# Loading q and k two batches ahead and transposing them with the DMA crossbar

**Chip, cores, metric.** One core of one Trainium2 chip. The metric is device time of one launch in microseconds (us), median of several runs.

## The reference

Two stages: attention in a window of 32 tokens on either side, with 8 global tokens, and a feed-forward layer on its result.

```python
# q, k, v: (8 batches, 8 heads, 576 tokens, 64)
scores = scale * (q @ k^T)                       # scale = 1/8
mask = (|i - j| <= 32) | is_global[i] | is_global[j]
attn = softmax(where(mask, scores, -1e9))
x = (attn @ v).transpose(0, 2, 1, 3).reshape(4608, 512)
h = x @ w_in                                     # 512 -> 2048: "first layer"
s = sin(alpha * h)
g = h + s * s / (alpha + 1e-9)
out = g @ w_out                                  # 2048 -> 512: "second layer"
```

## The kernel before

It goes through the batches in a loop. **Part p** is the attention of batch p, with the second-layer matmuls of token chunk p-1 as filling between its steps. **First-layer part p** follows: the 16 slots of the first layer of chunk p, each 4 matmuls, a sine on ScalarE, a square and an add. What the next batch needs is prepared in the meantime:

- GpSimd (called POOL in the profile) issues the loads of q, k and v of batch p+1 early in part p; `with_extra` hangs four on each of the first steps.
- TensorE transposes q and k of batch p+1, head pair by head pair, during the later attention steps of part p. VectorE copies transposed k and ScalarE copies transposed q out of PSUM, the memory that TensorE writes to.
- Sync, in slot 10 of first-layer part p, shifts v: it copies v within SBUF into a second arrangement and adds the rows of the global tokens. The V matmuls of part p+1 read that. Below, "the shift" stands for these four DMAs, two shifts and two copies of global v. `VW` has two buffers: the loads of v issued in part p fill the one that the V matmuls of part p do not read.

```python
def shift_v(b, eng=nc.sync):
    W = VW[b % 2].rearrange("p a h u d -> p a h (u d)")
    eng.dma_start(out=W[0:64, 1], in_=W[QB : QB + 64, 0])
    eng.dma_start(out=W[64:KB, 1, :, 0 : (NU - 1) * D], in_=W[64 - QB : KB - QB, 0, :, D:])

def global_v(b):
    # ... two more Sync DMAs into the same VW, from VgX

def T_half(src, b, hp, out):                      # TensorE transposes, one head pair
    for jt in range(NTW):
        for t, pr in heads:
            nc.tensor.transpose(out=out[pr, jt * TW : (jt + 1) * TW],
                in_=src[:, 2 * hp + t, jt, :], identity=identb[0:TW, 0:TW])

# ... the loop over p, part p:
    at = {2 + hp: [T_(p + 1, hp)] for hp in range(NHP)}
    parts = attention(p, psA, at)
    if p + 1 < B:
        with_extra(parts, load_slots(p + 1), 0, 4)
        # ... gathers and copies of the global tokens on GpSimd
    run(parts, counts, fill)
# ... first-layer part p:
    m1 = mm1(p, H2[p], psB, sq_last if p == B else sq_first if p == 0 else sq_late)
    vs = [partial(shift_v, p + 1), partial(global_v, p + 1)]
    m1[10] = partial(chain, m1[10], *vs)
```

`sq_late` says which engine squares which slot; nearly all are on GpSimd.

The softmax here doesn't subtract the row's maximum and nothing guards it: scores larger than these inputs give would overflow.

## Time and profile before

| | before |
|---|---|
| time, median | 359.7 us (358.81 to 361.65, 4 runs; the 360.4 of the prediction is the median of the first 3) |
| TensorE busy | 94% of the profiled span of 356.8 us |
| parts 2 to 6 (from the load of the Exp table to the first `hb` matmul) | 21.9 us each (part 4: 23.3, with an idle moment of 1.2 us in it) |
| first-layer parts 2 to 6 | 14.8 to 15.1 us each |

The prediction below reads the page. One thing that it uses is not shown there: when Sync shifts v, and when the result is needed. The timeline lists, for a group of instructions on one engine, start, duration, engine, line, operation, operands and count; a bracket at the end would be idle time of the engine ahead of it and what released it. First Sync in first-layer part 5, then TensorE early in part 3:

```profile
227.82 0.55 SPq L143 DMA_DIRECT2D VW<-VW  x1
228.43 0.66 SPq L144 DMA_DIRECT2D VW<-VW  x1
229.13 1.60 SPq L152 DMA_DIRECT2D VW<-VgX  x2
```

```profile
133.94 1.04 PE L703 MATMUL o<-w_out,H2b 128*128 128x512 bf16 x4
134.91 0.44 PE L553 MATMUL num<-E,VW 120*64 120x56 bf16 x16
```

The first V matmul (`num<-E,VW`) comes about 5 us into its attention part.

### The profile page before, as it was taken

How to read it: one execution, taken by the hardware profiler on the slowest of the kernel's cores; microseconds unless marked ns; L12 is line 12 of the kernel's file. 1: busy time of each engine (PE TensorE's matmuls, PEld its weight loads, DVE VectorE, ACT ScalarE, POOL GpSimd, SP SyncE). 2: the span in 40 equal slices, each digit the busy share in tenths (PEclk: the TensorE clock that was granted, in tenths of full speed). 3: DMA queues.
4: the chain of work that ended last, by engine and by line, in shares of the span. 5: the costliest groups of instructions: out<-in, count | busy, mean ns of one | idle time of the engine just before them, and what ended most of it. 6: DMA issues, size and time to landing. Idle time of an engine off the chain costs nothing.

```text
span 356.8 us, 9407 instructions
## 1 busy us (share of the span) xinstructions
PE 336.7 (94%) x3738; PEld 172.0 (48%) x3738; DVE 237.4 (67%) x527; ACT 245.9 (69%) x376; POOL 205.6 (58%) x302
## 2 busy tenths in 40 slices
PE   6686997999999999999989999999999999999996
PEld 5563444444455445544554446444544444444444
DVE  5765784758775687668764878487848764875610
ACT  3756885847894889578975888488848884844401
POOL 9858897355871787169805791579247205755000
PEclk9999999999999999999999999999999999999999
DMA  9999999940598429940995099409931001001012
GB/s 75 166 196 184 199 170 179 182 136 20 35 171 104 112 17 168 122 114 3 165 115 134 2 121 154 136 8 90 181 105 43 30 32 61 0 2 59 31 59 88
DMA packets 133149, 35.39 MB, mean 99 GB/s; under 512 B 121794, under 2 KB 126818, under 8 KB 133106
## 3 DMA queue, kind: packets, MB, share of 16 engines
q0 software_dynamic: 123120, 20.04, 77.5%
q1 hardware_dynamic: 9682, 14.63, 13.9%
q8 instruction: 29, 0.48, 0.5%
q10 hardware_dynamic: 304, 0.14, 0.1%
q14 instruction: 14, 0.11, 0.1%
HBM read 38.95 MB, written 9.44 MB: 136 GB/s over the span
## 4 chain that ended last, share of the span: by engine, by line
PE 65%; ACT 13%; DMA 7%; POOL 6%; issue 4%; DVE 3%; POOLq 1%; ACTq 0%; DVEq 0%
PE hb L664 28%; PE o L703 12%; PE ops L703 12%; DMA w_out<-in_moe_w_out_dram 4%; ACT E L507 3%; PE num L553 3%; PE Sp L501 2%; DVE H2b L654 2%; ACT L607 2%; PE den L535 2%; DMA QS<-in_q_dram 2%; PE hb L703 2%; ACT Sb L671 2%; ACT lnd L541 2%; ACT L614 2%
## 5 line engine op out<-in xcount | busy, mean ns | idle before, releaser
L671 ACT ACTIVATE Sb<-hb,alphaT 128x512 bf16<-128x512 f32 x144 | 96.9, 684 | 57.6 <-PE hb L664 54.2
L664 PE MATMUL hb<-xT,w_in 128*128 128x512 bf16 x576 | 128.9, 379 | 1.6 <-POOL xT L588 1.4
L681 POOL TENSOR_TENSOR S<-Sb 128x512 bf16<-128x512 bf16 x94 | 96.0, 1041 | 48.2 <-ACT Sb L671 44.8
L654 DVE SCALAR_TENSOR_TENSOR H2b<-S,recipT,hb 128x512 bf16<-128x512 bf16 x144 | 102.4, 740 | 30.7 <-POOL S L681 30.3
L664 PEld LDWEIGHTS <-w_in 128*128 128x128 bf16 x576 | 55.7, 98 | 68.3 <-issue 1.8
L703 PEld LDWEIGHTS <-H2b 128*128 128x128 bf16 x560 | 49.6, 98 | 56.6 <-issue 2.5
L703 PE MATMUL ops<-w_out,H2b 128*128 128x512 bf16 x304 | 73.9, 380 | 1.5 <-DMA w_out<-in_moe_w_out_dram 1.5
L703 PE MATMUL o<-w_out,H2b 128*128 128x512 bf16 x224 | 54.4, 381 | 0.0
L588 POOL COPY xT<-xg 128x4 bf16 x64 | 12.9, 201 | 66.1 <-DVE xg L586 62.6
L507 ACT ACTIVATE E<-Sp 128x896 bf16<-128x896 f32 x48 | 43.5, 905 | 7.1 <-PE Sp L501 7.0
L572 DVE TENSOR_TENSOR xT<-num,rec 128x384 bf16<-128x384 f32 (+1 forms) x60 | 25.9, 453 | 23.1 <-PE num L553 18.3
L541 ACT ACTIVATE lnd<-den 128x384 f32<-128x384 f32 x48 | 23.7, 493 | 17.8 <-PE den L535 17.6
L513 DVE TENSOR_TENSOR E<-E,MASK 128x896 bf16<-128x896 bf16 x48 | 30.0, 626 | 6.4 <-ACT E L507 6.4
L553 PEld LDWEIGHTS <-VW 120*64 120x64 bf16 (+1 forms) x768 | 16.7, 114 | 20.0 <-issue 12.5
L543 ACT ACTIVATE rec<-lnd 128x384 f32<-128x384 f32 x48 | 25.1, 524 | 1.5
L501 PE MATMUL Sp<-qT,kTw 64*128 64x56 bf16 x768 | 19.7, 189 | 5.5 <-ACT qT L421 2.1
L465 DVE COPY kTw<-Kps 128x1344 bf16<-128x1344 bf16 x29 | 24.3, 839 | 0.0
L681 DVE TENSOR_TENSOR S<-Sb 128x512 bf16<-128x512 bf16 x34 | 17.6, 517 | 9.9 <-ACT Sb L671 9.8
L501 PEld LDWEIGHTS <-kTw 64*128 64x128 bf16 x768 | 15.4, 96 | 17.4 <-issue 11.5
L553 PE MATMUL num<-E,VW 120*64 120x56 bf16 (+1 forms) x720 | 20.3, 197 | 1.4 <-issue 1.2
L128 POOL DMA_DIRECT2D KS<-in_k_dram x18 | 20.7, 1152 | 0.6 <-issue 0.6
L128 POOL DMA_DIRECT2D QS<-in_q_dram x18 | 20.2, 1122 | 0.0
(133 smaller groups left out, 304.1 us busy)
## 6 DMA issues: line engine op xcount, KB each, us to landing
out_dram<-osb SPq DMA_DIRECT2D x35, 256.0 KB
KS<-in_k_dram POOLq DMA_DIRECT2D x14, 288.0 KB, 5.6
QS<-in_q_dram POOLq DMA_DIRECT2D x14, 288.0 KB, 10.2
VW<-in_v_dram POOLq DMA_DIRECT2D x12, 336.0 KB, 11.4
VW<-VW SPq DMA_DIRECT2D x7, 384.0 KB
w_in<-in_moe_w_in_dram POOLq DMA_DIRECT2D x2, 1024.0 KB, 15.3
w_out<-in_moe_w_out_dram POOLq DMA_DIRECT2D x2, 1024.0 KB, 16.0
VW<-VW SPq DMA_DIRECT2D x7, 240.0 KB
```

What stands on the lines that cost most here:

```text
L128: nc.gpsimd.dma_start(out=dst[:, h0 : h0 + nh].rearrange("p h t d -> p (h t) d"), in_=heads_ap(src, b, h0, 0, TW, 0, nh * NTW),)
L501: nc.tensor.matmul(out=Sp[:, t, m * QC : (m + 1) * QC], lhsT=kTw[hp][pr, i, :], rhs=qT[hp][pr, i, :], start=True, stop=True, skip_group_ch ...
L507: nc.scalar.activation(out=E[:], in_=Sp[:, :, 0:EW], func=AF.Exp, scale=scale)
L513: nc.vector.tensor_tensor(out=E[:], in0=E[:], in1=mk[:, None, :].to_broadcast([P, 2, EW]), op=ALU.mult)
L541: nc.scalar.activation(out=lnd[:], in_=den[:, :, 0:QB], func=AF.Ln)
L553: nc.tensor.matmul(out=num[pr, m, :], lhsT=W[0:nk, i % 2, 2 * hp + t, i // 2, :], rhs=E[0:nk, t, m * QC : (m + 1) * QC], start=b > 0 or m ...
L572: nc.vector.tensor_tensor(out=xT[:, hp, x0 : x0 + nb * QB].rearrange("p (u c) -> p u c", u=nb), in0=num[:, m0 : m0 + nb, 0:QB], in1=rec[:, ...
L654: nc.vector.scalar_tensor_tensor(out=H2b[:, n_, :], in0=s_[:], scalar=recipT[:, n_ : n_ + 1], in1=h_, op0=ALU.mult, op1=ALU.add,)
L664: nc.tensor.matmul(out=h2[:], lhsT=w_in[:, ci, nt * P : (nt + 1) * P], rhs=xT[:, ci, c * CH : (c + 1) * CH], start=(ci == 0), stop=(ci == ...
L671: nc.scalar.activation(out=Sb[:], in_=h2[:], func=AF.Sin, scale=alphaT[:, nt : nt + 1])
L681: eng.tensor_tensor(out=S2[:], in0=Sb[:], in1=Sb[:], op=ALU.mult)
L703: nc.tensor.matmul(out=ops[:], lhsT=H2b[:, nt, ts * P : (ts + 1) * P], rhs=w_out[:, nt, :], start=(nt == 0), stop=(nt == NT - 1),)
```

## The change

Its intent is to take 384 transposes off TensorE in parts 3 to 6. q and k of batches 4 to 7 are loaded two batches ahead in 12 loads of 96 tokens; Sync transposes them through the DMA crossbar (a DMA that transposes what it copies) in the first-layer part between; the attention steps of the part after then copy from SBUF. The v shift goes from slot 10 to slot 13, behind the transposes.

```diff
+    def x_loads(b):
+        # ... 12 GpSimd loads, one for each of k, q and each 96 tokens
+    def cross(b, kq, jt):
+        if jt == 0:
+            XT[kq] = qkp.tile([P, NHP, S], BF, name=("KS", "QS")[kq])
+        src = qk[b][1 - kq]
+        nc.sync.dma_start_transpose(
+            out=XT[kq][:, :, jt * TW : (jt + 1) * TW],
+            in_=src[:, jt].rearrange("p h d -> p (h d)"),
+        )
+    def stage_X(b, hp):
+        # ... three VectorE copies of transposed k, one ScalarE copy of transposed q
-                    at = {2 + hp: [T_(p + 1, hp)] for hp in range(NHP)}
+                    at = {2 + hp: [partial(stage_X, p + 1, hp) if p > 2 else T_(p + 1, hp)] for hp in range(NHP)}
-                    with_extra(parts, load_slots(p + 1), 0, 4)
+                    ld = load_slots(p + 1) if p < 3 else v_loads(p + 1, QUADS)
+                    if p > 1 and p + 2 < B:
+                        ld += x_loads(p + 2)
+                    with_extra(parts, ld, 0, 5)
-                    m1[10] = partial(chain, m1[10], *vs)
+                    if p > 1 and p + 2 < B:
+                        for i in range(2 * NTW):
+                            m1[1 + i] = partial(chain, m1[1 + i], partial(cross, p + 2, i // NTW, i % NTW))
+                    m1[13] = partial(chain, m1[13], *vs)
```

More of the change, by code (lines that the diff above doesn't have):

```diff
@@ L476, in T_Q, with rows @@
         return partial(copy, out=qT[hp][:, :, 0:QB], in_=Qps[:].rearrange("p (i c) -> p i c", c=QB))
+    XT = {}
+    def x_loads(b):
+        QS = qkp.tile([TW, NTW, H, D], BF, name="QS")
+        KS = qkp.tile([TW, NTW, H, D], BF, name="KS")
+        qk[b] = (QS, KS)
+        def rows(src, dst, jt):
+            nc.gpsimd.dma_start(
+                out=dst[:, jt],
+                in_=bass.AP(
+                    tensor=src.tensor, offset=src.offset + (b * H * S + jt * TW) * D,
+                    ap=[[D, TW], [S * D, H], [1, D]],
+                ),
+            )
+        return [partial(rows, s_, d_, jt) for s_, d_ in ((k, KS), (q, QS)) for jt in range(NTW)]
+    def cross(b, kq, jt):
[5 more added lines that the diff above has]
+            in_=src[:, jt].rearrange("p h d -> p (h d)"),
+        )
+    def stage_X(b, hp):
+        kx, qx = XT[0][:, hp], XT[1][:, hp]
+        base = kx[:, 0:1]
+        win = lambda i0, n: bass.AP(
+            tensor=base.tensor, offset=base.offset + i0 * QB - WIN,
+            ap=[list(base.ap[0]), [QB, n], [1, KB]],
+        )
+        nc.vector.tensor_copy(out=kTw[hp][:, 1 : NW - 1, 0:KB], in_=win(1, NW - 2))
+        nc.vector.tensor_copy(out=kTw[hp][:, 0, WIN:KB], in_=kx[:, 0 : KB - WIN])
+        nc.vector.tensor_copy(out=kTw[hp][:, NW - 1, 0 : KB - WIN], in_=kx[:, S - KB + WIN : S])
+        return partial(
+            nc.scalar.copy, out=qT[hp][:, :, 0:QB], in_=qx.rearrange("p (i c) -> p i c", c=QB)
+        )
     def stage_T(b, hp, pool, tag):
```

## The prediction

> **What bounds the kernel now.** I read the engine table first, then the chain of waits, then busy time by stretch. The kernel alternates parts: attention of batch p together with the second layer of token chunk p-1 ("part p"), then the first layer of chunk p ("first-layer part p"). The page says that TensorE is almost never idle and that most of the closing chain is its own work:
>
> ```profile
> PE 336.7 (94%) x3738; PEld 172.0 (48%) x3738; DVE 237.4 (67%) x527; ACT 245.9 (69%) x376; POOL 205.6 (58%) x302
> q0 software_dynamic: 123120, 20.04, 77.5%
> q1 hardware_dynamic: 9682, 14.63, 13.9%
> PE 65%; ACT 13%; DMA 7%; POOL 6%; issue 4%; DVE 3%; POOLq 1%; ACTq 0%; DVEq 0%
> ```
>
> So TensorE work taken out of a stretch in which it never waits is worth its own length, if no other engine then becomes the limit. The chain shows where parts begin (the Exp table load, L607, at 241.18 and 277.91) and where the first layer takes over (263.29 and 297.71). Busy time in part 6, which still makes transposed q, k for batch 7, and in part 7, which makes none:
>
> ```profile
> 241.18:263.29 22.11, 21.84 (x362) 11.65 (x361) 15.67 (x39) 16.91 (x26) 12.59 (x24) 1.00 1.44 122
> 277.91:297.71 19.80, 19.55 (x266) 9.25 (x264) 12.48 (x35) 14.65 (x22) 2.35 (x9) 1.00 0.12 42
> ```
>
> Columns: length, then busy PE, PE weight loads, DVE, ACT, POOL. 96 matmuls fewer, 2.29 us less TensorE time, 2.31 us less length: the part is TensorE-bound and the saving passes through. The chain of part 5 shows the unit of that cost, 12 transposes of k and 12 of q for one head pair:
>
> ```profile
> 214.16 0.26 PE Kps L456 x12
> 214.42 0.26 PE qp L456 x12
> ```
>
> 0.52 us for a pair, four pairs a batch: 2.1 us, which fits the 2.3. Last, GpSimd, because the change hangs more loads on it. In part 2:
>
> ```profile
> 93.52 1.27 POOL L128 DMA_DIRECT2D KS<-in_k_dram  x1
> 97.13 1.18 POOL L128 DMA_DIRECT2D QS<-in_q_dram  x1
> 98.29 2.57 POOL L109 DMA_DIRECT2D VW<-in_v_dram  x2
> 100.84 0.54 POOL L115 DMA_DIRECT2D VW<-in_v_dram  x1
> 105.58 0.26 POOL L448 COPY qT<-GT 128x96 bf16<-128x96 bf16 x1
> 111.82 0.46 POOL L588 COPY xT<-xg 128x4 bf16 x2 [5.97 <-DVE xg L586]
> 112.49 1.51 POOL L588 COPY xT<-xg 128x4 bf16 x6 [0.20 <-POOL xT L588]
> ```
>
> GpSimd issues 7 loads by 101.4, is free from 105.8, and waits 6 us for work. The last two lines are the global tokens' columns of xT; the compiled order shows that the first matmul of the first layer waits for GpSimd there. They end at 114.0, first-layer part 2 starts at 114.87: less than 1 us of room against them, 6 us against what lies before them on GpSimd.
>
> **What the Trainium skill says.** "VectorE: DVE Perf Modes", The three transpose paths, gives 390 ns for a 128x128 bf16 transpose on TensorE and 1309 ns through the DMA crossbar. The trace before has pipelined TensorE transposes of 96x96 (12 in 0.26 us of chain), far cheaper than its isolated figure, and no crossbar transpose. The same page, The perf-mode tier table, lets a bf16 copy run at four elements per cycle from SBUF and at most two from PSUM; the trace has only the PSUM case, 128x1344 in 0.84 us. "DMA: Bandwidth & Descriptors", Issuing engines are not separate DMA queues, says that all queues run on the same 16 engines; the page agrees in listing both kinds as shares of 16 engines (77.5% and 13.9%). The same page, DMA Transpose (X-bar), says the plain transpose is issued from Sync or Scalar only; the change uses Sync alone, and nothing of before shows its rate.
>
> **The change, part by part.**
>
> Removed: 384 transposes with their weight loads, in parts 3 to 6 (batches 4 to 7). Worth 4 x 2.3 = 9.2 us at most.
>
> Kept on other engines: the copies. ScalarE still copies q, 0.63 us a head pair, so ACT stays near 16.9 us in a part that is now to last about 20. In steps that hold Exp 0.9, Ln 0.5, Exp 0.5 and the copy 0.63 it needs 2.5 us where TensorE needs about 1.9; later steps have slack. I charge 0.4 us a part. VectorE: one 128x1120 copy, at twice the PSUM rate 0.84 x 1120/1344 / 2 = 0.35 us (estimate), and two 128x80 edges at about 0.19 (what its smallest tensor operations take): 0.73 against 0.84 us, no change. Net gain 1.9 x 4 = **7.6 us**.
>
> Added on GpSimd: a batch's q, k in 12 loads of 768 rows for 4 loads of 2304. A load of 2304 rows takes 1.2 us to issue and one of 128 takes 0.54, so one of 768 about 0.73: 8.8 us for 4.7, in parts 2 to 5 instead of 3 to 6. Part 2 has both: q, k, v of batch 3 and then q, k of batch 4, 19 loads for 7. The compiled order shows that each software-queue DMA waits on one of 8 semaphores, so on the DMA eight before it. The first 7 loads (14,720 rows) keep the engines busy from about 96 to 111 us, 1.02 us per 1000 rows; a new load is then 0.78 us, and they land at 111.7, 112.5 and so on. The 12th waits for the 4th (114.1) and is issued by 115.2; then come the two gathers, which wait for the 5th and 6th (1.2 us each, to 118), 8 copies of 0.26 (to 120), and only then the 8 xT copies (2.04 us, to 122). First-layer part 2 can then start near 122 instead of 114.87: **+7 us**, once. In parts 3 to 5 there are 15 loads, v first; the same count frees GpSimd about 16 us into the part, and xT is needed about 17 us in: close, but hidden.
>
> Added on Sync: 12 crossbar transposes of 96x512 a batch, in first-layer parts 2 to 5, in front of the two v shifts and the two copies of global v (measured 3.5 us of issue). Sync is free at the start of such a part; the part lasts 14.6 us, and the first V matmul of the next comes 5.1 us later (134.91 against 129.77), so 19.7 us are to be had. 12 t + 3.5 + about 2 for landing and start fits if t is below about 1.2 us. From the skill's 1309 ns for a third of the size, mostly fixed cost I assume, I take t = 1.3 (estimate): 21 us, **1.4 us late in each of 4 parts, +5 us**, with a wide error. The move of the v shifts from slot 10 to 13 costs nothing itself, since Sync had started them 1.3 us into the part.
>
> Removed waits: the loads no longer race with the transposes of the same part; but in those parts these waits do not show, so 0.
>
> Sum: 360.4 - 7.6 + 7 + 5 = 364.8; I shade it to **364**.
>
> **The rivals.**
> - *TensorE saving passes through whole.* For it: part 7. It needs GpSimd unhurried in part 2 and t below 1.2. Time: 360.4 - 7.6 = 353. Against it: the eight-semaphore limit and the order on GpSimd.
> - *GpSimd becomes the bound of part 2 alone.* For it: the count above. With fast transposes: 360.
> - *Sync becomes the bound.* The transposes delay the v shifts, and V matmuls wait in parts 3 to 6. Each 0.1 us on t beyond 1.2 adds 1.2 x 4 = 4.8 us; t = 1.8 gives about 390. For it: isolated crossbar transposes are slow by the skill. Against it: 96 KB is little data, and successive ones can overlap.
> - *ScalarE holds the shortened parts.* ACT 16.9 of 19.8 us: it can take back 1 us a part, 4 in all.
>
> **Range and chances.** 353 needs everything hidden; t near 1.7 gives 385. The unknown t has its tail to the slow side. Over 2% faster means below 353.2, practically the whole gain with no new wait: 0.10. Over 2% slower means above 367.6, t about 1.4 or more: 0.38. Within: 0.52.
>
> **What would show it.** Parts 4 to 6 (Exp table load to first hb matmul) at about 20 us before any V wait, not 22.1; PE waiting on POOL xT at the start of first-layer part 2, about 7 us; the DVE copy at 0.35 to 0.45 us; Sync's transposes at 1.3 us apart and the v shift after them about 16 us into the part; V matmuls waiting for the DMA of VW for about 1.4 us. The prediction is wrong if the transposes take 0.8 us or 2, if the new loads land faster than 0.78 us each, or if part 2 shows no POOL wait.

## More of the kernel before

The experiments were run in several groups, each on one chip with its own runs of the kernel before (359 to 362 us); every ratio and difference below is against the runs of the same group unless said otherwise. Two traces compared by part are compared by the lengths of their parts.

Sync begins to issue the shift within the first 2 us of the first-layer part and the DMA engines are idle again some 4.5 us after its first line.

## The result, and the profile after

| | before | after |
|---|---|---|
| time, median of 4 runs | 359.7 us (358.81 to 361.65) | 390.69 us (388.2 to 393.21) |
| ratio | | 1.085 (95%: 1.077 to 1.094) |
| profiled span | 356.8 us | 388.1 us |

A ratio here is the mean time of one kernel's fast runs over that of the other's of the same rounds, so it is not quite the ratio of the medians. The change makes the kernel 8.5% slower, outside the predicted range of 353 to 385 us.

The page after: engine table, the granted TensorE clock in tenths by slices of a fortieth of the span, and the closing chain by engine:

```profile
PE 339.4 (87%) x3354; PEld 165.8 (43%) x3354; DVE 234.0 (60%) x559; ACT 246.2 (63%) x376; POOL 223.9 (58%) x334
...
PEclk9556999999995899999599977999699999999999
...
PE 51%; DMA 17%; POOL 10%; ACT 9%; issue 7%; DVE 5%; SPq 0%; POOLq 0%; ACTq 0%; DVEq 0%
```

384 instructions are gone, and yet TensorE is busy for longer than the 336.7 us of before. The clock row says why: before, every slice of it was 9. The dip at the very beginning, in which part 0 and 1 are prepared, is of no account: part 2 begins at 92.70, before at 92.83, and other runs have it or lack it. The four later ones are the subject. DMA was 7% of the chain and is 17%; GpSimd went from 6% to 10%.

By stretches (length; busy PE, PE weight loads, DVE, ACT, POOL with counts; granted clock; two DMA columns), parts 3 to 6:

```profile
141.06:161.04 19.98, 19.70 (x266) 9.24 (x263) 14.81 (x47) 16.94 (x26) 17.17 (x32) 1.00 1.61 136
175.81:204.83 29.02, 22.05 (x265) 10.04 (x264) 14.62 (x47) 16.95 (x26) 16.59 (x32) 0.82 1.35 126
219.61:250.63 31.02, 21.09 (x266) 9.72 (x263) 14.63 (x47) 16.94 (x26) 17.48 (x32) 0.83 1.32 121
265.40:294.44 29.04, 21.46 (x265) 9.92 (x264) 14.73 (x47) 16.94 (x26) 7.94 (x20) 0.88 0.65 85
```

Part 3 is what was hoped for: 19.98 us for 21.88. Parts 4 to 6 have the same TensorE work (265 or 266 matmul records; part 6 has fewer GpSimd operations) and take 9 to 11 us more. TensorE's timeline has the reason, one line for first-layer part 2 and one for each of parts 4 to 6:

```profile
123.66 7.68 PE L705 MATMUL hb<-xT,w_in 128*128 128x512 bf16 x24 [8.45 <-POOL xT L629]
...
187.78 0.70 PE L594 MATMUL num<-E,VW 120*64 120x56 bf16 x16 [6.76 <-DMA VW<-in_v_dram]
...
234.57 0.70 PE L594 MATMUL num<-E,VW 120*64 120x56 bf16 x16 [9.75 <-DMA VW<-VgX]
...
278.02 0.70 PE L594 MATMUL num<-E,VW 120*64 120x56 bf16 x16 [7.41 <-DMA VW<-in_v_dram]
```

One wait for GpSimd, 8.45 us, and three for v, 23.9 us together. The profile puts two of the three down to the loads of v and one to the copy of global v; the experiments will show that all three are the shift. (The loads of v fill the other `VW` buffer.) Sync ahead of the first of them:

```profile
162.19 7.74 SPq L500 DMA_TRANSPOSE KS<-KS  x6
170.03 7.70 SPq L500 DMA_TRANSPOSE QS<-QS  x6
177.79 0.62 SPq L143 DMA_DIRECT2D VW<-VW  x1
178.46 0.67 SPq L144 DMA_DIRECT2D VW<-VW  x1
179.18 2.17 SPq L152 DMA_DIRECT2D VW<-VgX  x2
```

Twelve transposes in 15.5 us, 1.29 us each; then the shift, 2 us after part 4 began at 175.81. GpSimd had begun to issue the loads of v at 176.50. The V matmul follows 10.0 us after the shift's first line. For parts 5 and 6 the same distance is 11.8 and 10.6 us (shift at 222.75 and 267.42).

GpSimd in part 2, ahead of the first wait:

```profile
109.54 0.77 POOL L486 DMA_DIRECT2D KS<-in_k_dram  x1 [1.29 <-DMA VW<-in_v_dram]
...
112.71 4.58 POOL L486 DMA_DIRECT2D QS<-in_q_dram  x6 [2.40 <-DMA VW<-in_v_dram]
...
121.57 2.04 POOL L629 COPY xT<-xg 128x4 bf16 x8
```

Each bracket is GpSimd waiting for an earlier load to land before it issues the next. It is through with the loads at 117.3, then come gathers and small copies, and the eight xT copies for which TensorE waits end at 123.6.

Last, the granted clock in stretches of 1 us around the first wait for v (the clock is the third number from the end):

```profile
182.00:183.00 1.00, 0.00 (x0) 0.00 (x0) 0.00 (x0) 0.00 (x0) 1.00 (x2) 1.00 1.56 157
...
184.00:185.00 1.00, 0.00 (x0) 0.00 (x0) 0.00 (x0) 0.00 (x0) 0.00 (x0) 0.50 1.56 208
...
191.00:192.00 1.00, 1.00 (x19) 0.56 (x18) 0.15 (x1) 0.00 (x0) 1.00 (x3) 0.50 2.39 164
...
194.00:195.00 1.00, 1.00 (x36) 0.64 (x33) 0.59 (x2) 0.47 (x2) 0.85 (x5) 1.00 2.49 153
```

TensorE stops at about 181, the clock halves at about 183, work goes on at 187.8, and the clock is whole again at about 193.3. The Trainium skill, "TensorE: Matmul & The Clock Gate", What's actually happening, says that an idle window of some 3.4 us puts the array at half rate until some 3.4 us of sustained work; the trace agrees on the half (0.50), with about 2 us to the fall and 5.5 us to the return here. Read the same way in steps of 0.5 us, the four dips of this trace have 2.0 to 4.6 us from the last matmul to the fall and 3.1 to 5.5 us from the next one to the return. So such a wait costs more than its own length.

**Where the 31 us came from.** Length of each stretch after minus before, and its terms. The clock's share is what is left of a part over 19.98 us (part 3) and the wait, and all of the growth of first-layer part 2, whose first 4.8 us run at a clock of 0.50:

| stretch | after - before | of it wait | half clock | TensorE saving |
|---|---|---|---|---|
| part 2, first-layer part 2 | +9.08, +2.34 | 8.45 for xT | 2.3 | - |
| part 3 | -1.90 | 0 | 0 | -1.9 |
| part 4 | +5.76 | 6.76 for v | 2.3 | -3.3 (with the idle moment of before) |
| part 5 | +9.08 | 9.75 for v | 1.3 | -2.0 |
| part 6 | +7.09 | 7.41 for v | 1.7 | -2.0 |
| sum | +31.45 | 32.4 | 7.6 | -9.1 |

The terms add up to 30.9; the other 0.6 us lie in part 2 and are not explained. The other first-layer parts agree within 0.01 us, and the spans differ by 31.3.

### The profile page after: what moved, and what is told of

It reads as the page before. It is cut to its first block, busy times and chain, and to the rows that moved or that the text cites. A ratio compares the mean times of both kernels' runs of the same rounds, so it can differ in the third digit from the quotient of the medians.

```text
span 388.1 us, 8838 instructions
## 1 busy us (share of the span) xinstructions
PE 339.4 (87%) x3354; PEld 165.8 (43%) x3354; DVE 234.0 (60%) x559; ACT 246.2 (63%) x376; POOL 223.9 (58%) x334
## 4 chain that ended last, share of the span: by engine, by line
PE 51%; DMA 17%; POOL 10%; ACT 9%; issue 7%; DVE 5%; SPq 0%; POOLq 0%; ACTq 0%; DVEq 0%
PE hb L705 20%; PE ops L744 11%; PE o L744 9%; DMA VW<-in_v_dram 9%; POOL S L722 4%; DMA w_out<-in_moe_w_out_dram 4%; PE num L594 3%; DVE H2b L695 3%; ACT E L548 3%; DMA VW<-VgX 3%; PE den L576 2%; ACT Sb L712 2%; DMA QS<-in_q_dram 2%; PE hb L744 2%; PE Sp L542 2%
## 5 line engine op out<-in xcount | busy, mean ns | idle before, releaser
L705 PE MATMUL hb<-xT,w_in 128*128 128x512 bf16 x576 | 131.9, 385 | 8.7 <-POOL xT L629 8.4
L744 PE MATMUL o<-w_out,H2b 128*128 128x512 bf16 x224 | 57.2, 395 | 0.0
L594 PE MATMUL num<-E,VW 120*64 120x56 bf16 (+1 forms) x720 | 21.5, 203 | 23.9 <-DMA VW<-in_v_dram 14.2
L594 PEld LDWEIGHTS <-VW 120*64 120x64 bf16 (+1 forms) x768 | 18.3, 121 | 44.0 <-issue 22.8
L486 POOL DMA_DIRECT2D QS<-in_q_dram x24 | 18.6, 787 | 12.0 <-DMA VW<-in_v_dram 9.1
L542 PE MATMUL Sp<-qT,kTw 64*128 64x56 bf16 x768 | 20.4, 193 | 5.8 <-ACT qT L421 2.3
L722 DVE TENSOR_TENSOR S<-Sb 128x512 bf16<-128x512 bf16 x34 | 17.5, 516 | 9.4 <-ACT Sb L712 9.4
L486 POOL DMA_DIRECT2D KS<-in_k_dram x24 | 18.6, 792 | 7.0 <-DMA VW<-in_v_dram 3.9
L576 PE MATMUL den<-E,ones 120*64 120x448 bf16 x96 | 19.8, 406 | 0.7 <-DVE E L554 0.4
## 6 DMA issues: line engine op xcount, KB each, us to landing
VW<-in_v_dram POOLq DMA_DIRECT2D x12, 336.0 KB, 10.9
```

Source lines behind the costliest of these rows:

```text
L486: nc.gpsimd.dma_start(out=dst[:, jt], in_=bass.AP(tensor=src.tensor, offset=src.offset + (b * H * S + jt * TW) * D, ap=[[D, TW], [S * D, H ...
L542: nc.tensor.matmul(out=Sp[:, t, m * QC : (m + 1) * QC], lhsT=kTw[hp][pr, i, :], rhs=qT[hp][pr, i, :], start=True, stop=True, skip_group_ch ...
L576: nc.tensor.matmul(out=den[pr].rearrange("p u c -> p (u c)"), lhsT=ones[0 : KB + NG], rhs=E[0 : KB + NG, t, :], start=True, stop=True, ski ...
L594: nc.tensor.matmul(out=num[pr, m, :], lhsT=W[0:nk, i % 2, 2 * hp + t, i // 2, :], rhs=E[0:nk, t, m * QC : (m + 1) * QC], start=b > 0 or m ...
L705: nc.tensor.matmul(out=h2[:], lhsT=w_in[:, ci, nt * P : (nt + 1) * P], rhs=xT[:, ci, c * CH : (c + 1) * CH], start=(ci == 0), stop=(ci == ...
L722: eng.tensor_tensor(out=S2[:], in0=Sb[:], in1=Sb[:], op=ALU.mult)
```

## The experiments

**Theory:** the late v shift makes the waits of parts 4 to 6, and the order on GpSimd makes that of part 2; both are a matter of order. **Rivals:** the v loads (which the profile names) make the waits; the transposes' own traffic makes them; the transposed q and k come late themselves. Each diff is against the changed kernel unless said otherwise.

### The shift ahead of the transposes

```diff
+                    m1[0] = partial(chain, m1[0], *vs)
                     # ... the 12 transposes in slots 1 to 12
-                    m1[13] = partial(chain, m1[13], *vs)
```

> The v shifts and the copies of global v are put on Sync ahead of the 12 crossbar transposes instead of behind them; nothing else changes. Theory (Sync's order, the shift issued 16 us into the first-layer part, then slow to land): the three waits before the first V matmul of parts 4, 5 and 6 (6.8, 9.8 and 7.4 us, 24 in all) go, and with them the stretches at half the granted clock after each; the wait on GpSimd at the start of first-layer part 2 (8.4 us) stays. 390.7 - 24 - about 7 for the clock = 360 us (357 to 364). Rival (the V matmuls wait for the v loads that the profile names, not for the shifts): the three waits stay and the time stays near 390. Rival (transposes slow down TensorE's other inputs): some wait moves elsewhere, 375.

Measured: 365.29 us (362.44 to 366.05) against 359.44 (358.43 to 360.61), ratio 1.014 (1.008 to 1.020). No V matmul waits any more; the first one of part 4 has no bracket:

```profile
179.84 0.44 PE L594 MATMUL num<-E,VW 120*64 120x56 bf16 x16
```

The v loads were untouched, so it was the shift and not they, and the transposes still ran, so their traffic alone does not make the waits. The last rival, late q and k, falls for the changed kernel by its own trace, where no copy of transposed q or k has idle time ahead of it; here it comes true once. Parts 4 and 6 are at 21.4 and 20.4 us. Part 5 is at 23.5, because now the transposes come late; ScalarE's copy of q there:

```profile
225.08 0.67 ACT L684 COPY qT<-QS 128x576 bf16<-128x576 bf16 x1 [2.65 <-DMA QS<-QS]
```

The q transposes had been issued from 208.8 to 215.7; the last of them landed 9.1 us after its issue, with loads under way. The rest of the loss, the wait for xT, stays (7.9 us). The total is a little above the upper end of what was expected, for the new wait.

### The v loads of part 6 later

```diff
-                    with_extra(parts, ld, 0, 5)
+                    with_extra(parts, ld, 0 if p < 6 else 7, 5)
```

> The changed kernel with one thing moved: in part 6 only, the three v loads of batch 7 are issued about 7 us into the part instead of at its start, so the v shift of batch 6, which Sync issues about 2 us into the part, has the DMA engines to itself. Theory 1 (the shift is late AND is slowed by the load burst, 10.6 us from issue to landing where 4.5 us do without a burst): the wait before the first V matmul of part 6 falls from 7.4 us to 1 to 2.5 us; parts 4 and 5 keep about 7 and 10. About 382 to 386 us. Theory 2 (only the late issue, or the transposes' own backlog in the DMA queue, makes the wait): part 6 keeps about 7 us, time near 390.

Measured, one look: 387.68 us against 359.44. Sync issues the shift for part 6 at 268.13, and TensorE waits 4.14 us instead of 7.41:

```profile
275.44 0.70 PE L594 MATMUL num<-E,VW 120*64 120x56 bf16 x16 [4.14 <-DMA VW<-VgX]
```

Issue to V matmul: 7.3 us for 10.6. Loads beside the shift thus account for 3.3 us of it in part 6, and 7.3 remain; parts 4 and 5 keep their waits (7.36 and 10.72 us). The run lies between the two expectations and leaves open how much of the 7.3 is due to transposes that are still under way. That was taken up in the last three runs.

### The loads of batch 4 spread over part 2 and first-layer part 2

```diff
+    sq_two = # ... fewer squares on GpSimd in first-layer part 2
+                    xl = x_loads(p + 2) if p > 1 and p + 2 < B else []
+                    if p > 2: ld += xl
+                    if p == 2: parts[7] = partial(chain, parts[7], *xl[:4])
+            if p == 2:
+                for i, f in enumerate(xl[4:]): m1[i] = partial(chain, m1[i], f)
```

> The changed kernel with the 12 loads of batch 4's q, k spread out: four after GpSimd's copies of the globals in part 2, eight between its squares in first-layer part 2, one of those squares per two slots moved to VectorE. Theory (19 loads in part 2, throttled by the 8 semaphores, hold up GpSimd's xT copies): TensorE's wait of 8.4 us at the start of first-layer part 2 goes to under 1 us; the V waits of parts 4 to 6 stay (24 us). About 380 us. Rival (xT is late for another reason, or GpSimd then falls behind in first-layer part 2): the wait stays or 4 to 8 us of waiting for POOL's squares take its place, 386 to 391.

Measured, one look: 388.3 us against 359.44: a miss. The wait for xT went from 8.45 us to nothing and part 2 from 31.0 to 22.2 us, as expected. But first-layer part 2 took 18.88 us for 17.40 (TensorE waits there for the adds of VectorE that follow the squares), part 3 got a wait for v of 2.20 us because its transposes start 17.5 us ahead of it instead of 24.5, and part 5 waited 10.39. What one stretch gained others gave back. Part 3 had been without a wait in the changed kernel only because Sync began its transposes at 116.52, during TensorE's wait for GpSimd.

### Both repairs

The edits of the first and the third experiment together.

> Both edits together: v shifts first, batch 4's loads spread. If the two waits and the clock drops after them were the whole loss, what is left is the TensorE saving: parts 3 to 6 at about 20 us for 22.1, so 360 - 8 = 352 us (350 to 355), over 2% faster than the kernel before. Rival (contention moves elsewhere, ScalarE bounds the shortened parts): 357 to 362.

Measured: 358.67 us (356.69 to 360.01) against 359.44, ratio 0.996 (0.991 to 1.0005). A miss by 6 to 7 us, inside the range of the rival: no large wait of TensorE is left, but there are small ones. In part 4 GpSimd waits 4.5 us for a load that must land, ScalarE for transposed q, and TensorE, in first-layer parts 2 and 4, for what they hold up:

```profile
182.22 0.67 ACT L684 COPY qT<-QS 128x576 bf16<-128x576 bf16 x1 [0.85 <-DMA QS<-QS]
```

```profile
131.83 1.89 PE L705 MATMUL hb<-xT,w_in 128*128 128x512 bf16 x8 [1.68 <-DVE H2b L695]
...
192.02 3.18 PE L705 MATMUL hb<-xT,w_in 128*128 128x512 bf16 x14 [1.27 <-POOL xT L629]
```

Parts 4 to 6 stand at 21.1 to 22.2 us, so the saving of 1.9 us is in part eaten. The transposes need an early place too, and so the shift must leave the first-layer part altogether.

### The shift inside the attention part, ahead of its last step

On top of the run before:

```diff
+                if 1 < p < B - 1:
+                    parts[8] = partial(chain, partial(shift_v, p + 1), partial(global_v, p + 1), parts[8])
-                    m1[0] = partial(chain, m1[0], *vs)
+                    if p == 1: m1[0] = partial(chain, m1[0], *vs)
-                            m1[1 + i] = ...  # transposes
+                            m1[i + 2] = ...
```

> On top of both repairs (v shift not behind the transposes, batch 4's loads spread): the v shift is issued by Sync in the last step of the attention part, where Sync idles, so the transposes start with the first-layer part instead of 3.5 us into it. Theory (parts 4 to 6 still take 21.1 to 22.2 us, not 20, because the late end of the transposes meets the next part's loads: ScalarE waits 0.9 us for transposed q, GpSimd 5 us for loads to land, TensorE 0.6 to 1.3 us for xT): parts 4 to 6 fall to about 20.4 us, first-layer part 2 stays at 18.9; 358.7 - 4 = 354.5 us. Rival (ScalarE's q copies or VectorE hold the parts): they stay at 21 to 22, 358.

Measured, one look: 356.86 us against 362.24 for the kernel before on the same chip. Parts 4 to 6 are at 20.6, 20.5 and 19.9 us, the clock at 1.00, as the theory has it; the time expected had been set on the level of the first runs, where the kernel before took some 3 us less. With shift and transposes both early, neither makes a large wait.

### The squares of first-layer part 2

On top of that:

```diff
-    sq_two = # slots 3, 7, 9, 13, 15 on VectorE, 5, 12 on ScalarE, the rest on GpSimd
+    sq_two = # slots 3, 7, 11, 15 on VectorE, other odd ones on ScalarE, even ones on GpSimd
```

> As the run before, with the squares of first-layer part 2 shared out again: GpSimd 8, ScalarE 4, VectorE 4 for 9, 2, 5. Theory (the eight loads put into that part, 6.3 us of GpSimd, made GpSimd and VectorE its bound, 18.9 us where it takes 14.8 elsewhere): it falls to about 16.5 us; 352 us. Rival (the part waits for something else): it stays at 18.9.

Measured, one look: 354.2 us against 362.24. First-layer part 2 is at 16.64 us for 18.88, which is most of the gain: GpSimd, which issues eight loads there, had been the limit of that part.

### Three loads later in parts 3 to 5

On top of that, the last three q loads go behind the xT copies:

```diff
-                        ld += xl
+                        ld += xl[:9]
-            if p == 2:
-                for i, f in enumerate(xl[4:]):
+            if 1 < p and p + 2 < B:
+                for i, f in enumerate(xl[4:] if p == 2 else xl[9:]):
```

> As the run before, and in parts 3 to 5 the last three q loads go behind GpSimd's xT copies, into the first-layer part. Theory (TensorE still waits about 1 us for xT because GpSimd issues 15 loads, held by the 8 semaphores, before it): the waits for xT in parts 4 to 6 go, parts at 20.0 us; 351 to 353 us, over 2% faster than the kernel before. Rival (GpSimd loses in the first-layer parts what it gains): first-layer parts grow from 14.8 to 15.5 or more, 354 to 356.

Measured: 360.08 us (359.61 to 360.69) against 362.24 (361.15 to 365.28), ratio 0.993 (0.987 to 0.999): a miss, and slower than the run before it. The parts are at 20.0 us, but first-layer parts 3 to 5 went from 14.8 to 16.9 us, each with a wait like this:

```profile
168.18 1.67 PE L705 MATMUL hb<-xT,w_in 128*128 128x512 bf16 x7 [1.42 <-DVE H2b L695]
```

GpSimd, busy with loads, squares later, and TensorE is held through the adds. The rival was right in kind; the time is above its range too.

### The loads alone, without the crossbar

The loads two ahead stay; the transposes are TensorE's, as in the kernel before.

```diff
-    at = {2 + hp: [partial(stage_X, p + 1, hp) if p > 2 else T_(p + 1, hp)] ...
+    at = {2 + hp: [T_(p + 1, hp)] for hp in range(NHP)}       # reads the new load layout
-    m1[1 + i] = partial(chain, m1[1 + i], partial(cross, p + 2, i // NTW, i % NTW))
```

> The changed kernel's loads alone: q, k of batches 4 to 7 load two batches ahead in the 12-load form, but are still transposed on TensorE; no crossbar transposes at all. Theory (GpSimd's share of the loss is the wait in part 2 and the half clock after it, about 11 us; Sync's share needs the transposes): 8 us of waiting for POOL at the start of first-layer part 2, parts 3 to 6 at 22 us with no V wait, 359.5 + 11 = 370 us. Rival (the load burst slows the v shift by itself): V waits of several us in parts 4 to 6, 385.

Measured, one look: 370.57 us against 362.24. The wait of part 2 is there in full, and no V matmul waits:

```profile
124.33 1.01 PE L705 MATMUL hb<-xT,w_in 128*128 128x512 bf16 x2 [8.06 <-POOL xT L629]
```

So the cost of the loads is separable. Part 2 and first-layer part 2 grow by 8.2 and 2.7 us against the trace before; the total grew by 8.3. (The two do not add up to it, as the trace before is of another group, whose kernel before took some 3 us less.) Parts 3 to 6 are at 21.9 to 23.0 us, as before: they lack the saving and the waits alike.

### The best of them, timed

The kernel of the experiment with the squares, in five rounds.

> The same program as the squares run, timed in five rounds for an interval. That run had one time, 354.2 us beside a median of 362.2 before it on that chip. If the repairs free the TensorE saving (parts 3 to 6 at 20.2 us for 22.3 on average, 8 us; first-layer part 2 gives back 1.6, part 2 up to 1.4), the ratio is 0.978 to 0.987, and the interval lies below 1. Rival (that one run was a lucky one, at a granted clock of 1.0 throughout): 0.99 to 1.0.

Measured: 355.09 us (354.59 to 356.35) against 361.47 (360.91 to 362.54), ratio 0.983 (0.981 to 0.985). It beats the kernel before by 1.7% and the changed one by far more. Parts 3 to 6 take 20.1 to 20.8 us; the longest, part 4, at full clock:

```profile
168.76:189.53 20.77, 19.06 (x262) 9.25 (x263) 15.75 (x48) 16.93 (x26) 16.75 (x32) 1.00 1.70 160
```

### A late shift without any crossbar transposes

Against the run with the loads alone: a tiny Sync DMA that reads the output of slot 14 holds the shift back to where the changed kernel has it.

```diff
+            if n_ == 14 and 1 < c < 6:
+                nc.sync.dma_start(out=gate[:], in_=H2b[0:1, 14, 0:16])
-                    m1[13] = partial(chain, m1[13], *vs)
+                    v_at = 15 if 1 < p < 6 else 13
+                    m1[v_at] = partial(chain, m1[v_at], *vs)
```

> All loads two batches ahead as in the change, no crossbar transposes (TensorE transposes kept); the v shift is made to wait for the last slot of the first-layer part, so that Sync issues it about 2 us into the attention part, as in the changed kernel. Theory 1 (lateness beside the load burst makes the waits, the transposes' own data is no part of it): waits ahead of the first V matmul of about 7 us (6 to 10) in parts 4 and 5, about 7 in part 6 and several us in part 3 too; some 395 us. Theory 2 (transposes still under way are a large share of the landing time): these waits fall to 1 to 5 us; some 380 to 385 us. The wait of TensorE for xT in part 2, about 8 us, stays under both.

Measured, one look: 412.31 us against 361.46. Sync, then TensorE, around part 4:

```profile
190.28 0.61 SPq L701 DMA_DIRECT2D gate<-H2b  x1
191.06 0.56 SPq L144 DMA_DIRECT2D VW<-VW  x1
191.66 0.65 SPq L145 DMA_DIRECT2D VW<-VW  x1
```

```profile
201.95 0.70 PE L595 MATMUL num<-E,VW 120*64 120x56 bf16 x16 [8.18 <-DMA VW<-VgX]
```

Issue to V matmul is 10.9, 10.9, 11.5 and 11.0 us in parts 3 to 6, as long as in the changed kernel, though the program has no crossbar transpose. Part 3 now waits too. The second theory falls: the transposes delay the shift by standing ahead of it; a share of their data is not seen in this comparison. The total is higher than expected, since the part without a wait is gone and TensorE has its transposes back.

### The same, with no loads beside it in part 6

```diff
-                    with_extra(parts, ld, 0, 5)
+                    with_extra(parts, ld, 0 if p < 6 else 7, 5)
```

> The run before with the three v loads of batch 7 some 7 steps later in part 6: a late shift with neither transposes nor a load burst beside it there. If transposes still under way had a share in the 7.3 us that e2_v7_late took from the shift's issue to the V matmul, it falls here to about 5.5 us (5 to 6.3), a wait of some 2.5 us; if not, it is 7.3 again (6.8 to 7.8). Parts 3 to 5 keep waits of about 8 us.

Measured, one look: 411.79 us against 361.29. In part 6 the shift is issued at 291.33:

```profile
297.41 0.53 PE L595 MATMUL num<-E,VW 120*64 120x56 bf16 x16 [3.36 <-DMA VW<-VgX]
```

6.1 us from issue to V matmul, against 11.0 with the loads beside it. The load burst is thus worth 4.9 us here. Against the 7.3 us of the second experiment, where transposes preceded the shift, 1.2 us would be the transposes' part; it rests on one look each.

### The kernel before, with the shift late and nothing else

The same gate as above, in the kernel before:

> The kernel before, and nothing but the v shift held back to about 2 us into parts 3 to 6, beside the loads that this kernel always issues there. If lateness beside a burst of loads is the whole mechanism, parts 3 to 6 wait 5 to 9 us each ahead of their first V matmul and the clock halves: some 390 to 400 us. If the change's finer, earlier loads are needed for it, the waits are under 3 us: some 370 us.

Measured, one look: 403.42 us against 361.29. Parts 3 and 6 (parts 4 and 5 wait 8.93 and 9.24 us):

```profile
146.44 0.71 PE L554 MATMUL num<-E,VW 120*64 120x56 bf16 x16 [8.90 <-DMA VW<-VgX]
...
288.72 0.70 PE L554 MATMUL num<-E,VW 120*64 120x56 bf16 x16 [9.44 <-DMA VW<-VgX]
```

36.5 us of waits out of a kernel that had none, 11.6 to 12.2 us from issue to V matmul, with this kernel's own loads (seven coarse ones) beside it. This settles the cause: neither the finer loads nor the crossbar is needed, only that the shift is issued late, next to the loads of the next batch. GpSimd began to issue these 1.8 us before the shift in part 4 (1.3 us in the changed kernel), and both move their data at the same time. Lateness alone is a part of it: with no loads beside the shift the run above still waited 3.36 us. The kernel before never paid this because its shift ran in a first-layer part, when no load was under way.

## Why the prediction was wrong, point by point

- **TensorE saving, 1.9 us a part net: right.** Part 3 is 1.90 us shorter; the window of part 7 had shown how much a part without transposes needs. The rival that ScalarE would hold the shortened parts fell: 16.9 us busy in 19.98, and the part reaches that length.
- **VectorE copies: right in sum.** The 128x1120 copy takes 444 ns in the median (the prediction: 350 by estimate), with its two edges 0.80 us for a predicted 0.73. By the element that is 1.6 times as fast as the copy from PSUM of before (128x1344 in 0.84 us), not twice.
- **GpSimd in part 2, +7 us: right in mechanism, a little small.** New loads take 0.78 to 0.79 us each to issue (predicted 0.73; its 0.78 was the time that the DMA engines need for one), xT copies are done at 123.6 (predicted 122), the wait is 8.45 us. The wait that ended last on GpSimd was not the predicted one of the twelfth new load for the fourth, but that of the seventh for a load of v (2.40 us). The run with the loads alone has it in isolation.
- **Transposes at t = 1.3: right, in part by luck.** They are 1.29 us apart (1.5 for the six of k in first-layer part 4). But the 1.3 was the time of one isolated transpose of a third of the size, with fixed cost assumed, and the spacing of issues is another quantity: with loads beside it one landed 9.1 us after its issue. The shift is issued 16.8, 17.9 and 16.8 us after the first-layer part begins, where the prediction says about 16.
- **The failed step: "12 t + 3.5 + about 2 for landing and start", and from it "1.4 us late in each of 4 parts, +5 us".** The mechanism, Sync made late and V matmuls waiting, is right, and so are the room of 19.7 us and, nearly, t; the term after the transposes is mis-sized. From the shift's first issue to the V matmul the prediction has 3.5 + 2 = 5.5 us; it measured 10.0, 11.8 and 10.6; and the start, which the 2 us were to cover too, took another 1.2 us ahead of the first transpose. That is 6.8 to 9.8 us late, 23.9 in all instead of 4 x 1.4 = 5.6. The 3.5 had been read in a first-layer part, where the DMA engines are otherwise idle, and the 2 was an estimate; together they are about right for such a place: 6.1 us with no loads beside the shift. But 16.8 us after the start of the first-layer part is 2 us into the next part, and there the loads run: issue alone took 3.6 to 5.0 us, and issue to V matmul 10.6 to 12.2 us in the runs without any transpose. The prediction knew both facts, the time of the loads and that all queues share 16 engines, and did not put them together. The count of parts was off as well: part 3 was spared, by luck, by the GpSimd wait ahead of it.
- **An omission: the clock.** No step charged for what a wait of several us does to the granted clock. It cost 2.3 us after the wait for xT and 5.2 us after the three for v, 7.6 in all. The 2.20 us wait in part 3 of the third experiment left the clock at 1.00; the 3.36 us one with no loads beside the shift was followed by some 3 us at 0.50.
- **"Close, but hidden", of xT in parts 3 to 5: not quite.** The waits for v cover it in the changed kernel; in the repaired ones TensorE waits up to 1.3 us for xT there.
- **The range.** It took all its slow side from t, the quantity that turned out right. With the measured landing, 360.4 - 7.6 + 8.5 + 23.9 + 7.6 = 392.8, where 390.7 was measured.

Open: why a shift beside loads lands 5 us later. The traces show both in flight at once, and that the loads' absence removes it (11.0 to 6.1 us), but not which packet waits for which.

## What to carry to other kernels

A transfer's time from issue to landing belongs to the place in the program where it was measured; before moving it, look at which other transfers run at the new place. When a queue gets new work, put the transfer that is needed first ahead of it, and give it a place of its own: here the same crossbar transposes lose 8.5% in a wrong order and win 1.7% in a right one, with the loads of batch 4 spread and the squares shared out again. Charge a TensorE wait of several us with the half-clock time behind it: here 1.3 to 2.3 us for waits of 6.8 to 9.8 us.

## What the Trainium skill lacked or had wrong

- "VectorE: DVE Perf Modes", The three transpose paths, gives one figure for the crossbar, 1309 ns for 128x128. That page has no other size. Here Sync issues transposes of 96x512, three times the elements, every 1.29 us, so their rate does not follow from that figure scaled by the elements. Other pages give a bandwidth of crossbar transposes; none that was found gives a spacing of issues, or a time to landing beside loads (9.1 us here, once).
- "DMA: Bandwidth & Descriptors", Issuing engines are not separate DMA queues, says that DMAs from several engines interleave, and gives no size for what that does to a short copy: from the shift's issue to its use 6.1 us without loads beside it, 10.0 to 12.2 us with GpSimd's loads under way.
- No page that was found says how many loads GpSimd can have outstanding. In this program each waits on one of eight semaphores, and so for the load eight before it (in part 2 those that wait are released in turn by loads of q, k, q, v and v, the second to sixth of the part); with 19 loads there, this and what lies behind it made TensorE wait 8.45 us.
- "TensorE: Matmul & The Clock Gate", What's actually happening, has about 3.4 us both to the fall and to the return, lets the point vary by 500 ns either way, and explains that by a window that runs on its own. Here the four dips fell after 2.0 to 4.6 us of idle time and returned after 3.1 to 5.5 us of work with gaps: around its figure, but with a wider spread than it states. Each wait of 6.8 to 9.8 us cost 1.3 to 2.3 us on top.
